# A sliding-window attention with a gated network: w_out folded in quarters, more transposes given to the DMA queues

## The chip, the cores and the metric

One core of a Trainium2 chip runs the kernel. The metric is the device time of one execution in microseconds (us), the median of several runs. TensorE (PE) multiplies matrices, VectorE (DVE) and ScalarE (ACT) copy and compute element by element, GpSimd (POOL) issues the loads that change type from float32 to bfloat16, and SyncE (SP) issues plain transfers and DMA transposes. All transfers share 16 DMA engines. Matrix results land in PSUM and are copied from there to SBUF.

## The reference, cut to what matters

Four batches, eight heads, 768 positions, head size 64. Attention keeps the first four positions (the sinks) and a window of 128; its output, heads side by side, is a 3072 x 512 matrix x. Two projections of x are multiplied with each other, then go through two more matrices:

```
keep = is_sink | in_window
scores = np.where(keep, scale * q @ k.T, -1e9)
a = softmax(scores)
x = (a @ v).transpose(0, 2, 1, 3).reshape(B * S, H * D)
h = (x @ w1) * (x @ w2) @ w3
out = h @ w_out
```

w1 and w2 are 512 x 1024, w3 is 1024 x 1024, w_out is 1024 x 512.

## The kernel before, in words

**The fold.** w3 @ w_out is made once on the core, as w3o (1024 x 512), so that each token row costs one projection. For each of the eight 128-row blocks i of w3, task t3.i (L381) turns the block on TensorE, copies it to w3t, and tasks fm.i.n (L392) multiply it with a column half n of w_out and copy the result (tile pw) to w3o. Three w3 blocks come as raw float32 through SP (L162, the names say "ab" because they lie in that buffer); they are transposed in float32, in two halves of four. The other five and w_out come through POOL as bfloat16.

**Attention.** A unit is a batch b, a pair of heads r and a tile t of 256 rows. q and k have to be turned so that the head dimension lies on partitions: batch 0 on TensorE from a layout of row pairs (tpq, tpk, L240), batch 1 on TensorE (L219), batches 2 and 3 by DMA transposes issued on SP, one per 128 rows (tdq, tdk, L249). sc.b.r.t multiplies (L288), ACT takes the exponential, DVE multiplies with the mask; av.b.r.t multiplies with v (L322), DVE divides. The sinks' scores for all heads are made in one go (sp, L282) with the first unit of a tile: in batch 0 for each tile on its own (256 columns), in batches 1 to 3 once for tiles 1 and 2 together (512 columns). The attention output xn is turned to xT: on TensorE for batches 0 and 1 (xt, L339), by DMA transposes for 2 and 3 (xd, L349).

**Network.** g.b.c.dt.half multiplies xT with a 128-column block of w1 (half 0, ACT copies it) or w2 (half 1, DVE multiplies the two into ab), for a chunk c of 256 (batch 0) or 384 tokens (L362). p.b.m multiplies 128 rows of ab with w3o (L402), a copy goes to o_sb, one of three buffers, and SP stores it (L409). The last of all projections is cut into pieces of 256, 128 and 128 columns, which are copied and stored apart (L419 to L426).

**What sets the order.** Each engine works in program order. TensorE's order is the string PLAN, task by task. The order on ACT, DVE and SP is found while the kernel is built, by a small planner with fixed costs and arrival times for the loads; a task marked "any" goes to whichever of DVE and ACT it reckons free first. The loads on POOL are in the list `order`, with the making of the identity matrices and masks between them (at places 2, 6 and 8 of the list); at most eight of POOL's loads are under way. Ahead of the first load TensorE multiplies zeros (keep_busy, tile pz), so many times as the planner sees room for. Every instruction waits for semaphores of what it reads, and everything behind it on its engine waits with it. PSUM has four buffers for all tasks but scores, which have two of their own.

```
order = [("wo", 256, 512), ("q", 0, 0), ("k", 0, 0), ("w3", 3), ("w3", 4), ("w3", 6), ("wo", 0, 256), ...
for n in (0, 1) if i < HALVED else (None,):
    me = ("fm", i, n)
    n0, n1 = (0, DM) if n is None else (256 * n, 256 * n + 256)
```

Of the kernel before, what the change touches and what calls it, by code (L numbers as in the profile page):

```python
# [21 lines left out]
def kernel(  # L22
# [31 lines left out]
    XPOSE = (2, 3)  # L54
    X_XPOSE = (2, 3)
# [3 lines left out]
    RAW = (("w3", 0), ("w3", 1), ("w3", 2))  # L59
# [62 lines left out]
    def load(what, *i):  # L122
# [18 lines left out]
        else:  # L141
# [5 lines left out]
    order = [("wo", 256, 512), ("q", 0, 0), ("k", 0, 0), ("w3", 3), ("w3", 4), ("w3", 6), ("wo", 0, 256), ("k",  # L147
             0, 1), ("v", 0, 0), ("q", 0, 1), ("w3", 5), ("w3", 7), ("w1", 0, 256), ("k", 0, 2),
             ("v", 0, 1), ("w2", 256, 512), ("w2", 0, 256), ("q", 0, 2), ("w1", 256, 512), ("w2",
             512, 768), ("w1", 512, 768), ("w1", 768, 1024), ("w2", 768, 1024), ("v", 0, 2)] + [  # L150
# [3 lines left out]

    def raw(i):
        return ab[0][:].rearrange("p k s -> p (k s)")[:, i * 2048:(i + 1) * 2048].bitcast(FP32)

    raw_at = {}
    for n, x in enumerate(RAW):
        raw_at[x] = raw(n)  # L160
        if x[0] == "w3":
            nc.sync.dma_start(out=raw(n), in_=moe_w3[x[1] * P:(x[1] + 1) * P, :])  # L162
        else:
            nc.sync.dma_start(out=raw(n).rearrange("p (h x) -> p h x", h=H), in_=pairs({"q": q, "k": k}[x[0]], *x[1:]))
# [61 lines left out]
    def cast(x):  # L226

        dst = {"q": qN, "k": kN}[x[0]][x[1]]
        out = dst[:, 2 * x[2]:2 * x[2] + 2, :].rearrange("p i n -> p (i n)")
        (nc.vector.tensor_copy if x[0] == "k" else nc.scalar.copy)(out, raw_at[x])  # L230
        yield
# [180 lines left out]
    def project_pieces(b, m):  # L412
# [10 lines left out]
        for i, (n0, n1) in enumerate(PIECES):  # L423
            o_sb = work.tile([P, n1 - n0], FP32, tag=f"o_{i}", bufs=1, name="o_sb")
            (nc.scalar.copy if i == 1 else nc.vector.tensor_copy)(o_sb[:], pos[i][:])
            (nc.scalar if i == 1 else nc.sync).dma_start(out=out[t0:t0 + P, n0:n1], in_=o_sb[:])  # L426
# [13 lines left out]
    def pieces(what, *i):  # L440
        if what == "qkv":
            for kb in range(i[1], i[2]):
                for x in "kqv":
                    slow = 0.9 if i[0] in XPOSE and x != "v" else 0.0
                    yield 0.25 * 1.35 + slow * RATE, 256, [(x, i[0], kb)]
# [6 lines left out]
        elif what == "w3":  # L452
            yield 0.475, 4096, [("w3", i[0])]
        elif what == "wo":
            yield 1.03 * (i[1] - i[0]) / 256, 1024, [("wo", n) for n in range(i[0] // 256, i[1] // 256)]
        else:
            yield 1.03 * (i[1] - i[0]) / 512, 1024, [(what, n) for n in range(i[0] // P, i[1] // P)]

    streams = [[[0.8 + RAW_US * n + 1.2, 0.475 if x[0] == "w3" else 0.555, 4096 if x[0] == "w3" else 512,
                 [("raw",) + x]] for n, x in enumerate(RAW)],  # L460
# [32 lines left out]
    for key in arrive:  # L493
        if key[0] in ("k", "q", "v"):
            arrive[key] += (0.0, 0.3, 1.0, 4.0)[key[1]]
# [3 lines left out]
    XP_US, XX_US, LATE_US = 9.0, 7.5, 12.0  # L499
    PLAN = """  # L500
        t3.0.0 t3.0.4 t3.1.0 t3.1.4 t3.2.0 t3.2.4 fm.0.1 fm.1.1 fm.2.1 tpq.0.0.2 tpq.0.0.0 tpk.0.0.0
        tpk.0.0.2 t3.3.0 sc.0.0.0 sc.0.1.0 t3.4.0 fm.3.1 t3.6.0 sc.0.2.0 sc.0.3.0 fm.4.1 fm.6.1 fm.3.0
        fm.0.0 tpk.0.1.0 tpk.0.1.2 fm.4.0 sv.0 fm.1.0 av.0.0.0 av.0.1.0 fm.2.0 tpq.0.1.2 tpq.0.1.0
        t3.5.0 xt.0.0.0 av.0.2.0 sc.0.0.1 sc.0.1.1 av.0.3.0 fm.5.0 fm.5.1 t3.7.0 tpk.0.2.0 tpk.0.2.2
        sc.0.2.1 sc.0.3.1 fm.7.0 av.0.0.1 av.0.1.1 xt.0.2.0 fm.7.1 fm.6.0 xt.0.0.1 av.0.2.1 g.0.0.0.0
        g.0.0.0.1 av.0.3.1 g.0.0.1.0 g.0.0.1.1 g.0.0.2.0 xt.0.2.1 g.0.0.2.1 tpq.0.2.2 tpq.0.2.0
        g.0.1.1.0 g.0.1.2.0 g.0.1.0.0 g.0.1.0.1 sc.0.0.2 sc.0.1.2 g.0.1.2.1 g.0.1.1.1 g.0.0.5.0
        g.0.1.4.0 g.0.1.5.0 g.0.1.4.1 g.0.0.5.1 g.0.1.3.0 g.0.1.6.0 g.0.1.6.1 sc.0.2.2 sc.0.3.2 av.0.0.2
        av.0.1.2 g.0.1.3.1 g.0.1.5.1 g.0.0.4.0 tpk.1.0 g.0.1.7.0 g.0.0.6.0 g.0.0.4.1 xt.0.0.2 tpq.1.0
        av.0.2.2 g.0.0.3.0 g.0.1.7.1 sc.1.0.0 sc.1.1.0 sv.1 g.0.0.6.1 p.0.2 tpq.1.1 av.0.3.2 g.0.0.3.1  # L510
        g.0.0.7.0 g.0.0.7.1 sc.1.2.0 sc.1.3.0 xt.0.2.2 av.1.0.0 tpk.1.1 p.0.0 g.0.2.4.0 tpq.1.2
        g.0.2.5.0 g.0.2.1.0 g.0.2.1.1 av.1.1.0 p.0.1 av.1.2.0 g.0.2.4.1 g.0.2.2.0 av.1.3.0 g.0.2.2.1
        sc.1.0.1 sc.1.1.1 xt.1.2.0 g.0.2.5.1 g.0.2.3.0 g.0.2.7.0 g.0.2.7.1 g.0.2.0.0 g.0.2.0.1 g.0.2.3.1
        g.0.2.6.0 tpk.1.2 sc.1.2.1 sc.1.3.1 g.0.2.6.1 p.0.3 av.1.0.1 av.1.1.1 av.1.2.1 sc.1.0.2 sc.1.1.2
        p.0.5 xt.1.0.1 av.1.3.1 sc.1.2.2 sc.1.3.2 xt.1.0.0 p.0.4 xt.1.2.1 av.1.0.2 av.1.1.2 sc.2.0.0
        sc.2.1.0 av.1.2.2 g.1.0.4.0 g.1.0.4.1 xt.1.0.2 g.1.0.0.0 av.1.3.2 g.1.0.6.0 g.1.0.6.1 xt.1.2.2
        g.1.0.2.0 g.1.0.2.1 g.1.0.0.1 g.1.1.6.0 g.1.0.1.0 g.1.1.1.0 g.1.1.1.1 g.1.1.6.1 g.1.0.5.0
        g.1.0.5.1 av.2.0.0 av.2.1.0 sc.2.2.0 sc.2.3.0 g.1.0.1.1 g.1.0.3.0 g.1.0.3.1 g.1.1.7.0 g.1.1.7.1
        av.2.2.0 g.1.1.5.0 sc.2.0.1 sc.2.1.1 g.1.1.5.1 av.2.3.0 g.1.1.2.0 g.1.1.2.1 g.1.1.3.0 g.1.1.0.0
        g.1.1.0.1 g.1.0.7.0 g.1.0.7.1 sv.2 sc.2.2.1 sc.2.3.1 g.1.1.3.1 p.1.2 av.2.0.1 av.2.1.1 av.2.2.1  # L520
        g.1.1.4.0 g.1.1.4.1 av.2.3.1 sc.2.0.2 sc.2.1.2 p.1.4 p.1.3 sc.2.2.2 sc.2.3.2 av.2.0.2 av.2.1.2
        p.1.5 sc.3.0.0 sc.3.1.0 p.1.1 av.2.2.2 av.2.3.2 sc.3.2.0 sc.3.3.0 p.1.0 g.2.0.7.0 g.2.0.5.0
        g.2.0.5.1 g.2.0.2.0 av.3.0.0 g.2.0.2.1 g.2.0.7.1 g.2.0.4.0 g.2.0.4.1 g.2.0.1.0 g.2.0.1.1 sv.3
        g.2.0.3.0 g.2.0.3.1 g.2.0.6.0 g.2.0.6.1 av.3.1.0 sc.3.0.1 sc.3.1.1 g.2.1.3.0 g.2.1.3.1 av.3.2.0
        g.2.1.7.0 g.2.1.4.0 g.2.1.2.0 g.2.1.2.1 av.3.3.0 g.2.1.7.1 g.2.1.5.0 sc.3.2.1 sc.3.3.1 g.2.1.4.1
        g.2.1.1.0 g.2.1.1.1 g.2.1.6.0 av.3.0.1 av.3.1.1 sc.3.0.2 sc.3.1.2 av.3.2.1 av.3.3.1 g.2.1.5.1
        g.2.0.0.0 g.2.0.0.1 sc.3.2.2 sc.3.3.2 g.2.1.6.1 p.2.2 p.2.0 av.3.0.2 av.3.1.2 av.3.2.2 av.3.3.2
        g.2.1.0.0 g.2.1.0.1 p.2.1 p.2.5 g.3.0.5.0 g.3.0.5.1 g.3.0.0.0 g.3.0.6.0 g.3.0.3.0 g.3.0.0.1
        g.3.0.4.0 g.3.0.4.1 g.3.0.3.1 p.2.4 g.3.0.6.1 g.3.1.1.0 g.3.1.1.1 g.3.1.5.0 g.3.1.3.0 g.3.1.5.1
        g.3.1.6.0 g.3.0.1.0 g.3.0.1.1 g.3.1.6.1 g.3.1.3.1 g.3.1.0.0 g.3.1.0.1 g.3.1.7.0 g.3.1.7.1  # L530
        g.3.1.2.0 g.3.0.2.0 g.3.0.2.1 g.3.0.7.0 g.3.0.7.1 g.3.1.2.1 g.3.1.4.0 g.3.1.4.1 p.3.2 p.3.3
        p.3.4 p.3.0 p.3.1 p.3.5 p.2.3
    """

    def task(name, prio, gen, stages, after=(), loads=(), ring=None, started=(),
# [6 lines left out]
    w3_home = [{("t3", x[1], j): (2048 * n, 2048 * n + 2048) for n, x in enumerate(RAW) if x[0] == "w3"  # L542
                for j in (0, 4)}, {("t3", i, 0): (n * DF, n * DF + DF) for n, i in enumerate(BF_W3) if n < 6}]
    for n, x in enumerate(RAW):
        if x[0] != "w3":
            w3_home[0]["cast", x[0]] = (2048 * n, 2048 * n + 2048)
    for i in range(KFF):
# [9 lines left out]
        for n in (0, 1) if i < HALVED else (None,):  # L557
            me = ("fm", i, n)
            folded.append(me)
            n0, n1 = (0, DM) if n is None else (256 * n, 256 * n + 256)  # L560
# [3 lines left out]
                 t3, ([("wo", 0)] if n != 1 else []) + ([("wo", 1)] if n != 0 else []), "mm")  # L564
    def xn_free(b, t):
        b, t = (b, t - 2) if t == 2 else (b - 1, t + 1)
        return [] if b < 0 else ([("xd", b, t, i) for i in range(2)] if b in X_XPOSE else
# [3 lines left out]
    for b in range(B):  # L571
        for t in range(NT):
# [3 lines left out]
            for n, src, dst in (("k", kN[b], kT[b]), ("q", qN[b], qT[b])):  # L576
                if b in XPOSE:
                    for kb in kbs:
                        qk.append(("td" + n, b, kb))
                        task(qk[-1], 1, transposes_dma(src, dst, kb), [("sp", 1.4), ("dma", XP_US)],  # L580
                             war, [(n, b, kb)],
                             late=[("tp" + n, b - 2, t, r0) for r0 in (0, 2)] if b - 2 in PAIRED else
                             [("tp" + n, b - 2, t)])
# [11 lines left out]
                else:  # L595
                    qk.append(("tp" + n, b, t))
                    task(qk[-1], 1, transposes(src, dst, t), [("pe", 0.447), ("dve", 0.69)],
                         [], [(n, b, kb) for kb in kbs], "mm")
# [6 lines left out]
            for r in range(NP):  # L605
# [5 lines left out]
                if t > 0 and r == 0 and (b == 0 or t == 1):  # L611
                    sinks = (t, t + 1) if b == 0 else (1, NT)
                    after.append(("sk", b))
                    if b > 0:
                        after += [("tdq", b, 4), ("tdq", b, 5)] if b in XPOSE else [("tpq", b, 2)]
# [14 lines left out]
                if not lead and b not in X_XPOSE:  # L630
                    task(("xt", b, r - 1, t), 2.5, x_transposes(b, r - 1, t),
                         [("pe", 0.224), ("any", dict(dve=0.69, act=0.6))],
                         [("av", b, r - 1, t), ("av", b, r, t)], [], "mm")
            if b in X_XPOSE:
                for i in range(2):
                    task(("xd", b, t, i), 1, x_transposes_dma(b, t, i), [("sp", 1.3), ("dma", XX_US)],
# [209 lines left out]
```

## Time and profile before

| | us |
|---|---|
| median of 6 runs | 198.9 (198.12 to 199.43) |
| the profiled execution | 198.12 |
| its span in the trace | 196.4 |
| TensorE busy | 188.0 (96%) |
| VectorE, ScalarE busy | 117.2 and 102.6 |
| share of q0 (loads from POOL) of the 16 DMA engines | 91.7% |
| share of q1 (SP: raw loads, transposes, stores) | 30.9% |

The span runs from the first to the last instruction of the trace; the 1.7 us between it and the execution's time lie around it. Busy time counts overlapping instructions once. A line names source line, engine and operation, then what is written and read; "us to landing" is the time from a DMA's issue to its completion. The chain of work that ended last follows the last instruction back, at each step to what it waited for; its pieces are start, length and what ran.

### The profile page before, as it was taken

The page shows a single profiled execution, that of the slowest core. Times are in us where ns is not written, and L with a number is a line of the kernel's source. Part 1 is how long each engine was busy: PE and PEld are TensorE (multiplying, and loading weights), DVE is VectorE, ACT ScalarE, POOL GpSimd, SP SyncE. Part 2 cuts the span into 40 slices and gives each one's busy share as a digit, 9 for nine tenths or more (in the row PEclk, how much of TensorE's full clock was granted, in tenths as well). Part 3 has the DMA queues.
Part 4 walks back from the last instruction along what each step waited for, and adds up shares of the span by engine and source line. Part 5 has one row for each costly group of instructions (what it writes and reads, how often), then busy time and mean ns, then how long its engine had stood idle before and what let it go on. Part 6 is the DMA issues. An engine that isn't in the chain of part 4 may idle for free.

```text
span 196.4 us, 4629 instructions
## 1 busy us (share of the span) xinstructions
PE 188.0 (96%) x1858; PEld 125.8 (64%) x1870; DVE 117.2 (60%) x278; ACT 102.6 (52%) x174; POOL 71.9 (37%) x96
## 2 busy tenths in 40 slices
PE   6699999999999999999999999999999999999993
PEld 2577788888867686766655655556565655665442
DVE  5446477756887778684757766665687523254112
ACT  2338378468545477973566466526865332423210
POOL 7972666679999855242781000000000000000000
PEclk9999999999999999999999999999999999999999
DMA  6999999999999999999999999920212330100233
GB/s 216 234 199 194 182 185 186 197 170 155 155 154 181 180 145 158 152 205 146 155 155 132 156 168 245 154 80 0 29 27 73 118 134 0 58 0 0 104 146 124
DMA packets 99445, 26.77 MB, mean 136 GB/s; under 512 B 88928, under 2 KB 95456, under 8 KB 99424
## 3 DMA queue, kind: packets, MB, share of 16 engines
q0 software_dynamic: 75664, 13.90, 91.7%
q1 hardware_dynamic: 23616, 12.52, 30.9%
q8 instruction: 14, 0.23, 0.5%
q10 hardware_dynamic: 144, 0.07, 0.1%
q14 instruction: 7, 0.06, 0.1%
HBM read 29.36 MB, written 6.29 MB: 182 GB/s over the span
## 4 chain that ended last, share of the span: by engine, by line
PE 88%; DMA 6%; POOL 3%; issue 1%; DVE 0%; POOLq 0%
PE pg L362 43%; PE po L402 20%; PE av L322 8%; DMA wo_sb<-in_moe_w_out_dram 6%; PE sc L288 6%; PE pw L392 5%; PE xt L339 2%; PE tp L219 1%; PE tp L240 1%; PE po L419 1%; POOL ab L129 1%; PE sp L282 1%; POOL wo_sb L119 1%; PE tp L381 1%; PE vp L263 0%
## 5 line engine op out<-in xcount | busy, mean ns | idle before, releaser
L362 PE MATMUL pg<-xT,w_sb 128*128 128x384 bf16 (+1 forms) x576 | 89.7, 308 | 0.0
L362 PEld LDWEIGHTS <-w_sb 128*128 128x128 bf16 x576 | 54.2, 98 | 26.5 <-issue 1.3
L366 DVE TENSOR_TENSOR ab<-a_sb,pg 128x384 bf16<-128x384 f32 (+1 forms) x72 | 36.4, 509 | 34.7 <-PE pg L362 32.5
L369 ACT COPY a_sb<-pg 128x384 f32<-128x384 f32 (+1 forms) x72 | 31.9, 444 | 38.2 <-PE pg L362 28.4
L296 ACT ACTIVATE ex<-sc 128x1024 bf16<-128x1024 f32 (+1 forms) x48 | 43.9, 955 | 7.9 <-PE sc L288 7.7
L402 PE MATMUL po<-w3o,ab 128*128 128x512 bf16 x172 | 41.4, 379 | 0.6
L300 DVE TENSOR_TENSOR am<-ex,maskt 128x1024 bf16<-128x1024 bf16 (+1 forms) x48 | 29.8, 640 | 2.2 <-ACT ex L296 2.0
L402 PEld LDWEIGHTS <-ab 128*128 128x128 bf16 x184 | 17.5, 98 | 19.5 <-issue 0.5
L212 ACT COPY o_sb<-po 128x512 f32<-128x512 f32 x17 | 10.0, 585 | 23.0 <-PE po L402 22.9
L329 DVE TENSOR_TENSOR xn<-av,rec 128x256 bf16<-128x256 f32 x48 | 20.4, 424 | 1.6
L113 POOL DMA_DIRECT2D qN<-in_q_dram x18 | 16.1, 895 | 9.5 <-DMA vN<-in_v_dram 8.2
L113 POOL DMA_DIRECT2D vN<-in_v_dram x18 | 16.1, 892 | 8.6 <-DMA kN<-in_k_dram 7.1
L322 PE MATMUL av<-vN,am 128*128 128x65 bf16 x352 | 18.5, 193 | 0.0
L322 PEld LDWEIGHTS <-am 128*128 128x128 bf16 x352 | 16.8, 97 | 2.1 <-issue 0.2
L113 POOL DMA_DIRECT2D kN<-in_k_dram x18 | 16.1, 894 | 4.9 <-DMA qN<-in_q_dram 4.4
L392 PE MATMUL pw<-wo_sb,w3t 128*128 128x256 bf16 x128 | 15.6, 273 | 2.1 <-DMA wo_sb<-in_moe_w_out_dram 2.1
L392 PEld LDWEIGHTS <-w3t 128*128 128x128 bf16 x128 | 12.0, 98 | 4.3 <-DMA wo_sb<-in_moe_w_out_dram 1.7
L288 PE MATMUL sc<-qT,kT 64*128 64x128 bf16 (+1 forms) x256 | 13.9, 238 | 0.0
L326 DVE RECIPROCAL rec<-av 128x4 f32<-128x4 f32 x48 | 8.5, 177 | 8.0 <-PE av L322 7.6
L322 PE MATMUL av<-vs,es 128*128 128x130 bf16 x64 | 12.2, 220 | 0.0
L212 DVE COPY o_sb<-po 128x512 f32<-128x512 f32 x6 | 4.1, 692 | 11.9 <-PE po L402 8.8
L288 PEld LDWEIGHTS <-kT 64*128 64x128 bf16 x256 | 8.2, 94 | 4.5 <-issue 3.2
(70 smaller groups left out, 121.9 us busy)
## 6 DMA issues: line engine op xcount, KB each, us to landing
out_dram<-o_sb SPq DMA_DIRECT2D x23, 256.0 KB, 2.4
vN<-in_v_dram POOLq DMA_DIRECT2D x24, 128.0 KB, 9.5
kN<-in_k_dram POOLq DMA_DIRECT2D x18, 128.0 KB, 9.1
qN<-in_q_dram POOLq DMA_DIRECT2D x18, 128.0 KB, 9.5
w_sb<-in_moe_w_dram POOLq DMA_DIRECT2D x8, 256.0 KB, 9.6
ab<-in_moe_w_dram SPq DMA_DIRECT2D x3, 512.0 KB, 4.2
ab<-in_moe_w_dram POOLq DMA_DIRECT2D x5, 256.0 KB, 10.7
wo_sb<-in_moe_w_out_dram POOLq DMA_DIRECT2D x2, 512.0 KB, 10.5
```

The costliest lines, as they stand in the source:

```text
L113: nc.gpsimd.dma_start(out=dst, in_=rows(src, b, kb))
L212: (nc.scalar.copy if home[me] == "act" else nc.vector.tensor_copy)(dst, src)
L288: nc.tensor.matmul(sc[:, e, c:c + n], kT[b][hp, r, kb * P:(kb + 1) * P], qT[b][hp, r, qb * P:qb * P + n], start=True, stop=True)
L296: nc.scalar.activation(ex[:, :, c0:], sc[:, :, c0:], ACTF.Exp, scale=scale)
L300: nc.vector.tensor_mul(am[:, :, c0:], ex[:, :, c0:], mk)
L322: nc.tensor.matmul(o, lhs, rhs, start=(n == 0), stop=(n == len(todo) - 1), skip_group_check=True)
L329: nc.vector.tensor_mul(xns[b, t][:, :, r, :, :], av[:, :, :, 0:D], rec[:].to_broadcast([P, 2, 2, D]))
L362: nc.tensor.matmul(pg[:], w_sb[:, kk, dt * P:(dt + 1) * P], xT[b][:, kk, tk], start=(kk == 0), stop=(kk == NP - 1))
L366: nc.vector.tensor_mul(ab[b][:, dt, tk], gate_a.pop((b, c, dt))[:], pg[:])
L369: nc.scalar.copy(a_sb[:], pg[:])
L392: nc.tensor.matmul(po[:], w3T[i][:, j, :], wo_sb[:, j, n0:n1], start=(j == 0), stop=(j == KFF - 1))
L402: nc.tensor.matmul(po[:], ab[b][:, kk, m * P:(m + 1) * P], w3o[:, kk, :], start=(kk == 0), stop=(kk == KFF - 1))
```

## The change

Five things change together.

- w_out is loaded in four quarters of 128 columns (`CUTS`) instead of two halves, and each fold task fm.i.n makes 128 columns instead of 256: 32 tasks of 8 matmuls instead of 16. The functions that load, multiply and copy are the same; a path for loading w_out raw is added but not taken, as `RAW` is unchanged.
- Tile 2 (rows 512 to 767) of batch 1: q and k are turned by four DMA transposes on SP instead of 16 matmuls and two copies, and x by two DMA transposes instead of 8 matmuls and two copies.
- The sinks of batch 1 are made for tiles 1 and 2 apart, 256 columns each, as in batch 0.
- The list `order` and PLAN are others. The first loads are now two quarters of w_out and two w3 blocks; the first transposes are of the second raw w3 block; attention of batch 0 begins after more of the fold. The number of filler matmuls goes from 6 to 12: nine ahead of the first transposes, and three after the first fold task. The planner's arrival times and DMA costs are other numbers.
- In the last projection DVE copies the first two pieces and ACT the third (before: DVE, ACT, DVE), and the stores follow the three copies, two on SP and the third on ACT.

On SP the order becomes: three raw loads; the four transposes of batch 1; then transposes of batch 2 with stores of batch 0 between them; the two x transposes of batch 1 after batch 2's ninth q or k transpose; the last three of batch 2; then batch 3's with batch 1's stores and batch 2's x transposes.

```diff
-    XPOSE = (2, 3)
-    X_XPOSE = (2, 3)
+    XPOSE = [(1, 2), (2, 0), (2, 1), (2, 2), (3, 0), (3, 1), (3, 2)]
+    X_XPOSE = [(1, 2), (2, 0), (2, 1), (2, 2), (3, 0), (3, 1), (3, 2)]
+    CUTS = (0, 128, 256, 384, 512)
+    SPLIT = (0, 1)
...
-    order = [("wo", 256, 512), ("q", 0, 0), ("k", 0, 0), ("w3", 3), ("w3", 4), ("w3", 6), ("wo", 0, 256), ("k",
-             0, 1), ("v", 0, 0), ("q", 0, 1), ("w3", 5), ("w3", 7), ("w1", 0, 256), ("k", 0, 2),
...
+    order = [("wo", 384, 512), ("wo", 128, 256), ("w3", 5), ("w3", 4), ("wo", 0, 128), ("q", 0, 0), ("k", 0, 0),
+             ("w3", 3), ("wo", 256, 384), ("v", 0, 0), ("k", 0, 1), ("q", 0, 1), ("w3", 7), ("w3",
+             6), ("w1", 256, 512), ("q", 0, 2), ("k", 0, 2), ("v", 0, 1), ("w2", 256, 512), ("w1",
...
-        for i, (n0, n1) in enumerate(PIECES):
-            o_sb = work.tile([P, n1 - n0], FP32, tag=f"o_{i}", bufs=1, name="o_sb")
-            (nc.scalar.copy if i == 1 else nc.vector.tensor_copy)(o_sb[:], pos[i][:])
-            (nc.scalar if i == 1 else nc.sync).dma_start(out=out[t0:t0 + P, n0:n1], in_=o_sb[:])
+        o_sbs = [work.tile([P, n1 - n0], FP32, tag=f"o_{i}", bufs=1, name="o_sb") for i, (n0, n1) in enumerate(PIECES)]
+        for i in range(3):
+            (nc.scalar.copy if i == 2 else nc.vector.tensor_copy)(o_sbs[i][:], pos[i][:])
+        turn = (len(RAW) + 2 * 2 * len(XPOSE) + 2 * len(X_XPOSE) + B * NB - 1) % 8
+        for i in {7: (2, 0, 1), 6: (0, 2, 1), 5: (0, 1, 2)}.get(turn, (0, 1, 2)):
+            n0, n1 = PIECES[i]
+            (nc.scalar if i == 2 else nc.sync).dma_start(out=out[t0:t0 + P, n0:n1], in_=o_sbs[i][:])
...
     PLAN = """
-        t3.0.0 t3.0.4 t3.1.0 t3.1.4 t3.2.0 t3.2.4 fm.0.1 fm.1.1 fm.2.1 tpq.0.0.2 tpq.0.0.0 tpk.0.0.0
-        tpk.0.0.2 t3.3.0 sc.0.0.0 sc.0.1.0 t3.4.0 fm.3.1 t3.6.0 sc.0.2.0 sc.0.3.0 fm.4.1 fm.6.1 fm.3.0
...
+        t3.1.4 t3.0.4 t3.2.0 t3.0.0 t3.1.0 t3.2.4 fm.0.3 fm.1.1 fm.2.1 fm.2.3 t3.5.0 fm.0.1 fm.1.3
+        t3.4.0 fm.5.1 fm.5.3 fm.1.0 fm.4.0 fm.5.0 fm.2.0 fm.0.0 fm.4.1 tpq.0.0.0 tpq.0.0.2 tpk.0.0.2
+        tpk.0.0.0 fm.4.3 t3.3.0 sc.0.0.0 sc.0.1.0 fm.2.2 fm.5.2 sv.0 fm.3.0 fm.3.1 sc.0.2.0 sc.0.3.0
...
-        for n in (0, 1) if i < HALVED else (None,):
+        for n in range(len(CUTS) - 1):
             me = ("fm", i, n)
             folded.append(me)
-            n0, n1 = (0, DM) if n is None else (256 * n, 256 * n + 256)
+            n0, n1 = CUTS[n], CUTS[n + 1]
...
-                if b in XPOSE:
+                if (b, t) in XPOSE:
                     for kb in kbs:
...
-                if t > 0 and r == 0 and (b == 0 or t == 1):
-                    sinks = (t, t + 1) if b == 0 else (1, NT)
+                if t > 0 and r == 0 and (b in SPLIT or t == 1):
+                    sinks = (t, t + 1) if b in SPLIT else (1, NT)
...
-                if not lead and b not in X_XPOSE:
+                if not lead and (b, t) not in X_XPOSE:
                     task(("xt", b, r - 1, t), 2.5, x_transposes(b, r - 1, t),
...
-            if b in X_XPOSE:
+            if (b, t) in X_XPOSE:
                 for i in range(2):
```

## The prediction

> **What bounds the kernel now.** I read the page first, for which engine fills the span.
>
> ```profile
> span 196.4 us, 4629 instructions
> PE 188.0 (96%) x1858; PEld 125.8 (64%) x1870; DVE 117.2 (60%) x278; ACT 102.6 (52%) x174; POOL 71.9 (37%) x96
> PE   6699999999999999999999999999999999999993
> DMA  6999999999999999999999999920212330100233
> ```
>
> TensorE is full except in the first two slices and the last. The DMA engines are full as well, until about 130 us. The chain that ended last shows where each of the two sets the pace:
>
> ```profile
> 7.49 12.57 DMA wo_sb<-in_moe_w_out_dram
> 20.06 0.04 issue
> 20.10 1.91 PE pw L392 x16
> ...
> 51.32 0.22 PE xt L339 x4
> 51.55 0.45 PE tp L219 x8
> ...
> 67.17 0.33 PE sp L282 x4
> ...
> 72.31 0.55 PE sc L288 x12
> 72.86 0.54 PE pg L362 x4
> ...
> 191.29 1.78 PE po L419 x24
> ```
>
> From 20.10 us on the chain is TensorE alone, back to back, up to 193.07 us; a tail of 3.3 us (copy, store, landing) follows. So a microsecond of TensorE work taken out after 20 us is a microsecond of the end, as long as no new wait opens. Before 20 us the loads set the pace. TensorE's timeline there:
>
> ```profile
> 4.36 3.98 PE L381 MATMUL tp<-ident,ab 128*128 128x128 f32 x24 [0.29 <-DMA ab<-in_moe_w_dram]
> 9.84 2.79 PE L392 MATMUL pw<-wo_sb,w3t 128*128 128x256 bf16 x24 [1.51 <-DMA wo_sb<-in_moe_w_out_dram]
> 13.93 0.62 PE L381 MATMUL tp<-ident,ab 128*128 128x128 bf16 x8 [0.28 <-DMA ab<-in_moe_w_dram]
> 15.25 0.62 PE L381 MATMUL tp<-ident,ab 128*128 128x128 bf16 x8 [0.26 <-DMA ab<-in_moe_w_dram]
> 20.10 1.91 PE L392 MATMUL pw<-wo_sb,w3t 128*128 128x256 bf16 x16 [0.62 <-DMA wo_sb<-in_moe_w_out_dram]
> ```
>
> Four waits for loads, 2.67 us, the largest for the first half of w_out.
>
> **What the Trainium skill says.** "TensorE: Matmul & The Clock Gate", Part 1, gives one matmul every N/2.4 + 2.5 ns once warm and half the clock before that, with a warm-up of about 3.4 us of activity. The trace agrees: 24 matmuls of 16x128 and 8x256 columns take 1.78 us on the chain (55.6 and 109 ns each make 1.76), and 8 of the 24 fp32 transposes start between 4.30 and 6.05 us, 213 ns apart, the next ones 109 ns. "DMA: Bandwidth & Descriptors", Specifications, puts full rate at 512 bytes a transfer and more. Here q0 moved about 760 packets of 512 bytes in 16 to 18 us (380 a us) and 1427 mostly of 256 bytes in 10 to 12 us (714 a us): 195 against 183 GB/s, a small loss. "Advanced Engine Details and Errata", X-Bar Transpose, calls DMA transposes as fast as regular DMAs. For landing on a busy queue the trace decides: 8.2 and 8.5 us in 62 to 92 us, where plain loads take 12 to 14.
>
> **The change, part by part.**
>
> *Transposes of batch 1, last 256 rows.* TensorE loses 16 matmuls (tp L219, 0.45 per 8) and 8 (xt L339, 0.22 per 4): 0.90 + 0.44 = -1.34 us. Their copies leave DVE and ACT, neither of which is on the chain: nothing.
>
> *Sinks of batch 1 per tile.* One 512-column set of 4 (0.33) becomes two of 256 (0.22 each, the length that batch 0's has): +0.11 us; each holds one change of tile shape, about 0.1 us (0.55 against 0.44 for sc). Over the whole built order such changes go from 62 to 63, this one alone.
>
> *Fold in quarters.* 128 matmuls of 256 columns become 256 of 128: 256 x 55.6 - 128 x 109.2 = +0.26 us. Sixteen more PSUM copies, but 265 to 292 ns each on two engines (the last tile's 128-column copies) against one fold task per 0.44 us: hidden under TensorE; without that cover they would cost 16 x 0.28 = 4.5 us shared by two engines.
>
> So the work after the start shrinks by 1.34 - 0.11 - 0.26 = 0.97 us.
>
> *w_out in quarters, start.* POOL has two more loads to issue, about 0.9 us each; q0 is loaded 6 to 12 us deep by then, so that is hidden (bare, it would delay each later load by 1.8 us). A half takes 1024/380 = 2.7 us of queue time, a quarter 1024/714 = 1.43, so w_out takes 5.7 instead of 5.4, and loads behind it are 0.3 later. The three raw w3 blocks land 3.4, 4.2 and 5.4 us after their issues (4.2, 5.5, 7.1 us), and q0 hardly moves before 5.8 us (7 packets in 4.0 to 5.8). First quarter: about 8.6 us (half: 9.8). Then +1.43 for a quarter, q or k (q 11.2, k 12.7 now), +1.27 for a w3 block, +0.85 for v. In the new order: wo 8.6, wo 10.05, w3 11.3, w3 12.6, wo 14.05, q 15.5, k 16.95, w3 18.2, wo 19.65, v 20.5 and 21.3, up to 0.7 later at the end, as the second half is now.
>
> TensorE against this: nine filler matmuls end at 5.2 (six now at 4.07), and the first transposes need the second raw block: start 5.6 instead of 4.36. That is less bad than it looks, as only 2 or 3 then run cold instead of 8. Third block at 7.26 as now, transposes end at 9.1. One quarter (0.45), three fillers (0.64), then fm.1.1 at 10.15, w3 block 5 at 11.5, block 4 at 12.8, fm.1.0 at 14.15, q at 16.8, k at 17.5, block 3 about 18.8, first scores done at 19.8. At full clock that work is 24 x 0.109 + 120 x 0.056 + 24 x 0.056 + 1.1 + 0.55 = 12.3 us, so 7.5 us are lost, and with some 0.6 for the fourth quarter and v just behind, 8.1. Now, up to 20.10: 24 x 0.109 + 48 x 0.109 + 24 x 0.056 + 1.1 + 1.1 = 11.4, so 8.7 lost. Gain 0.6 us; with loads 0.7 us later than I take them it is nothing or slightly negative, with loads always ahead 1.2.
>
> *Last tile.* Same matmuls; ACT instead of DVE copies the last 128 columns (265 against 292 ns) and stores from its own queue, 1.7 us to landing on both. Nothing; bounds -0.1 to +0.3.
>
> *The DMA transposes and SP's queue.* SP now issues four transposes of batch 1 ahead of the first store, and two of x in the middle of batch 2's. Each costs SP 1.2 to 1.7 us. Batch 1's rows 512 to 767 landed from 56.2 (k) to 59.7 us (q); issued at 57 to 61, transposed by 70; the scores that read them come at about 74.5 on TensorE. Covered by 4 us. The stores of batch 0 wait behind them, but the first is ready only at 65. On the shared engines a transpose takes the place of about 0.75 us of loads (in 76 to 78 us q1 moved 726 packets, mostly of transposes, and q0 1108, against 2339 in 54 to 56 us: 1231 packets given up, 1.05 us, for 726; I take a transpose for 512 of 256 bytes, its 128 KB). So batch 2's loads end some 3 us later, batch 3's 4.5. Batch 2's last q transpose (issued 86.6, landed 94.4, first read at 99.1) also stands behind the two x transposes, which wait for attention of batch 1 at 84: I get 90.7 + 7.8 = 98.5, read at 101. Batch 2's second x tile, behind batch 3's k transposes: 113 + 6.5 = 119.5, read at 121.8 (now 120.3 and 123.8). Each cover shrinks from about 4 us to about 2.4. If both hold, nothing; if one fails by 1 or 2 us, that much is paid at once, because scores and gates stand in TensorE's fixed order with the projections behind them. I take 0.2 as the expected small loss.
>
> *The rest of the order.* Gates, scores and projections are dealt out anew, in the same shapes. I cost that at nothing: ACT and DVE, at 52 and 60%, hide it. If a copy stands in a wrong place, TensorE waits for it, 0 to 1 us in all; a gain is not to be had, since no wait of TensorE is left after 20 us to remove.
>
> **Sum.** 0.97 + 0.6 - 0.2 = 1.4 us: span 196.4 to 195.0, the profiled execution 198.12 to 196.7. It was the fastest of six; on the median 198.9 the same step gives 197.5 us, -0.7%. No change can be told within about 0.5%, 1.0 us.
>
> **Rivals.** *The start is bound by loads and gains nothing* (chance 0.28): several steps above come within 0.3 us of their landing. For it speaks that the second half of w_out took 3.6 us beyond its predecessor rather than 2.7; against it that q0's order now brings a usable piece every 1.3 us. Then 0.97 less some 0.5 of waits: 198.4 us. *The DMA transposes become the bound* (0.17): batch 2's last q transpose lands late at the first scores of its second tile. Cover 2.5 us; slower by more than 1.0 us needs a landing 2.5 + 1.4 + 1.0 = 4.9 us later than 98.5. For it speak 14.3 us to landing for loads in 62 to 92 us and a full DMA row; against it that loads are only half of what SP waits for. At 5.5 us late TensorE waits 3.0: 197.5 + 3.0 = 200.5 us. *The start runs free of loads and nothing stalls*: 0.97 + 1.2, 196.7 us, in the first case's range.
>
> **Chances and range.** The forecast, 0.55 (its own range 196.5 to 197.9); no gain at the start, 0.28; transposes bound, 0.17. Faster 0.55, same 0.28, slower 0.17. Range 196.6 to 200.0.
>
> **What would show it.** First fp32 transposes at 5.6 us, first fold matmul near 9.1, the waits between 9 and 22 us under 1.5 us in total; TensorE back to back from 22 us; a wait for qT or xT near 101 or 122 us would show the second rival. I am wrong if TensorE's work is not about 1 us smaller, if the quarters land later than 8.6 and 10, or if stores behind SP's transposes hold back the output copies.

## The result, and the profile after

The changed kernel takes 199.95 us (median of 20 runs, 198.66 to 203.16), the kernel before 198.71 (41 runs measured beside it). The ratio is 1.0049, 95% interval 1.0029 to 1.0068: about 1 us slower, where the prediction had 1.4 us faster. The profiled execution took 201.61 us with a span of 199.9, so it is one of the longer ones; what it shows is larger than in the median run. Ratios leave out executions more than 1.5% above the fastest of the same kernel and medians keep them: three executions of the changed kernel are left out, and below, 15 of 22 with batch 3's loads later and seven of 22 with the other start.

The page of the changed kernel, first the engines' shares in 40 slices of 5 us:

```profile
span 199.9 us, 4881 instructions
PE 190.2 (95%) x1973; PEld 127.2 (64%) x1984; DVE 118.6 (59%) x282; ACT 102.8 (51%) x183; POOL 73.8 (37%) x98
PE   7899999999999999999999997599999999999993
```

TensorE is full but for the first two slices, the last, and two from 120 to 130 us. The last two are new. TensorE's waits from 22 us to the end (total, times, longest) say what it waited for there:

```profile
PE pg L383 <- ACT o_sb L226: 2.1, 1, 2.1
PE pg L383 <- DMA xT<-xn: 1.0, 1, 1.0
```

The chain of work that ended last, in that place (start, length, what ran):

```profile
119.56 7.21 DMA out_dram<-o_sb
...
127.13 0.59 ACT o_sb L226
...
127.77 2.72 PE pg L383 x8
130.49 0.66 PE av L343 x12
```

A store that SP issued at 119.56 us landed 7.2 us later; ScalarE waited for it with a copy into the same output buffer, and TensorE waited for that copy. Just before, at 123.0, TensorE had already waited 1.0 us for xT of batch 2. Then eight gate matmuls take 2.72 us. The same piece takes 1.30 us in the kernel of 197.3 us below, so TensorE's clock had dropped to half: the granted clock is 0.50 from 127.75 to 131.10 us, and 1.00 before and after. The Trainium skill ("TensorE: Matmul & The Clock Gate", Part 1) says that an idle window of about 3.4 us halves the clock; here waits of 1.0 and 2.1 us were enough. Waits 3.1 and slow matmuls (2.72 - 1.30) + (0.66 - 0.37) = 1.7 make 4.8 us; these are called the hole below. Without them the span is 195.1 us, and 195.0 was predicted.

The clock does not fall in every execution. Of the 21 on record, six have a mean granted clock of 0.99, as this one; the other 15 have 0.998 or more and a median of 199.73 us. So the kernel is slower at full clock too. Median and ratio miss the prediction by 2.4 to 2.6 us; if all of that is the hole, it is usually about half of the one shown.

The start went nearly as foretold. TensorE's timeline there:

```profile
5.71 1.06 PE L402 MATMUL tp<-ident,ab 128*128 128x128 f32 x8 [0.56 <-DMA ab<-in_moe_w_dram]
7.21 1.97 PE L402 MATMUL tp<-ident,ab 128*128 128x128 f32 x16 [0.43 <-DMA ab<-in_moe_w_dram]
9.09 0.62 PE L413 MATMUL pw<-wo_sb,w3t 128*128 128x128 bf16 x8
...
20.54 0.84 PE L413 MATMUL pw<-wo_sb,w3t 128*128 128x128 bf16 x12 [0.36 <-DMA wo_sb<-in_moe_w_out_dram]
```

First fp32 transposes at 5.71 (5.6 predicted), first fold matmul at 9.09 (9.1); the five waits for loads of before, 2.96 us (the prediction's 2.67 leaves out the first), have become four of 1.61 us: these three, and 0.26 us for batch 0's first k at 17.9.

What is late in the hole is batch 2's second x tile. In the trace SP issued its two transposes at 116.39 and 118.20 us, and they landed at 124.01 and 125.44. Ahead of them SP stood until 115.10 for a k transpose of batch 3, whose load landed at 115.09; in the kernel before the same load landed at 105.22. SP's issues there, first before, then after (start, length, what):

```profile
108.42 1.34 SPq L249 DMA_TRANSPOSE kT<-kN  x1
...
113.22 4.50 SPq L349 DMA_TRANSPOSE xT<-xn  x2
```

```profile
115.10 1.19 SPq L270 DMA_TRANSPOSE kT<-kN  x1
116.39 3.08 SPq L370 DMA_TRANSPOSE xT<-xn  x2
119.56 0.53 SPq L430 DMA_DIRECT2D out_dram<-o_sb  x1
```

The first line of each is the transpose of that same load. The store that ScalarE's copy waited for had its data at 114.4 us, but stands right behind the x tile on SP, so both waits of the hole follow from SP's wait for the late load.

### The profile page after: what moved, and what is told of

Read it like the earlier page. It is cut to its first block, busy times and chain, and to the rows that moved or that the text cites. A ratio compares the mean times of both kernels' runs of the same rounds, so it can differ in the third digit from the quotient of the medians.

```text
span 199.9 us, 4881 instructions
## 1 busy us (share of the span) xinstructions
PE 190.2 (95%) x1973; PEld 127.2 (64%) x1984; DVE 118.6 (59%) x282; ACT 102.8 (51%) x183; POOL 73.8 (37%) x98
## 4 chain that ended last, share of the span: by engine, by line
PE 83%; DMA 9%; POOL 4%; issue 1%; ACT 1%; POOLq 0%; ACTq 0%
PE pg L383 42%; PE po L423 18%; PE av L343 7%; PE sc L309 6%; DMA wo_sb<-in_moe_w_out_dram 5%; PE pw L413 4%; DMA out_dram<-o_sb 4%; POOL wo_sb L121 1%; PE xt L360 1%; PE tp L261 1%; PE po L440 1%; PE tp L233 1%; POOL ab L131 1%; PE sp L303 1%; PE tp L402 1%
## 5 line engine op out<-in xcount | busy, mean ns | idle before, releaser
L383 PE MATMUL pg<-xT,w_sb 128*128 128x384 bf16 (+1 forms) x576 | 91.8, 311 | 3.1 <-ACT o_sb L226 2.1
L226 ACT COPY o_sb<-po 128x512 f32<-128x512 f32 x18 | 10.5, 585 | 25.9 <-PE po L423 19.4
L343 PE MATMUL av<-vN,am 128*128 128x65 bf16 x352 | 19.3, 195 | 0.0
L413 PE MATMUL pw<-wo_sb,w3t 128*128 128x128 bf16 x256 | 16.3, 219 | 0.4 <-DMA wo_sb<-in_moe_w_out_dram 0.4
L413 PEld LDWEIGHTS <-w3t 128*128 128x128 bf16 x256 | 14.6, 98 | 1.5 <-DMA wo_sb<-in_moe_w_out_dram 0.6
L226 DVE COPY o_sb<-po 128x512 f32<-128x512 f32 x5 | 3.5, 691 | 9.8 <-PE po L423 6.9
(69 smaller groups left out, 123.0 us busy)
```

The lines of the kernel that those rows point to most:

```text
L226: (nc.scalar.copy if home[me] == "act" else nc.vector.tensor_copy)(dst, src)
L343: nc.tensor.matmul(o, lhs, rhs, start=(n == 0), stop=(n == len(todo) - 1), skip_group_check=True)
L383: nc.tensor.matmul(pg[:], w_sb[:, kk, dt * P:(dt + 1) * P], xT[b][:, kk, tk], start=(kk == 0), stop=(kk == NP - 1))
L413: nc.tensor.matmul(po[:], w3T[i][:, j, :], wo_sb[:, j, n0:n1], start=(j == 0), stop=(j == KFF - 1))
```

## The experiments

The kernel before ran beside all of them: 198.7 to 199.0 us. Each ratio is to it, with its 95% interval. Theory and rival are named in each expectation.

**Six output buffers.**

```diff
-        o_sb = work.tile([P, DM], FP32, tag="o_sb", name="o_sb")
+        o_sb = work.tile([P, DM], FP32, tag="o_sb", bufs=6, name="o_sb")
```

> The changed kernel with six output buffers (o_sb) instead of three, nothing else; the order on every engine is the same. Theory A (batch 1's stores stand in SP's order behind transposes that wait for late loads, the three output buffers are all taken, ACT stops at a copy and the gates behind it stop TensorE): the copy no longer waits, the 4.5 us wait of ACT for a store is gone, what stays is about 1 us of waiting for xT of batch 2; span about 196 to 196.5, time 197.8 to 198.2, ratio to the kernel before 0.995 to 0.998. Theory B (xT of batch 2 is late because the DMA queues are full, and the output buffers only happen to be full at the same time): TensorE waits for xT as long as before, ratio 1.002 to 1.006.

Measured: 201.53 us, ratio 1.0114 (1.0061 to 1.0166). The wait for the output copy is gone; TensorE's waits after 22 us are now headed by

```profile
PE pg L383 <- DMA xT<-xn: 3.8, 2, 2.4
```

and 0.5 us for a gate's copy. The buffers only stood in front of the x tiles, which are late themselves. The second and the third x tile of batch 2 were each waited for. Whether more buffers made it slower than the change (1.0049, 1.0029 to 1.0068) is not certain, as the intervals touch; in this profile the start, too, was 1.2 us later.

**Batch 1's stores on ScalarE's queue.**

```diff
-        nc.sync.dma_start(out=out[t0:t0 + P, :], in_=o_sb[:])
+        (nc.scalar if b == 1 else nc.sync).dma_start(out=out[t0:t0 + P, :], in_=o_sb[:])
```

> The changed kernel with the six stores of batch 1 issued by ACT right behind their copies instead of by SP; SP's order is otherwise the same, and ACT spends about 0.4 to 0.5 us more per store. Theory A, with SP's order as the cause: stores leave within 1 us of the copy, land 6 to 7 us later, and the fourth copy (8 us after the first) finds a buffer; ratio 0.994 to 0.999. Theory A', with the long landing as the cause rather than SP's order: ACT still waits for 1 us or more, ratio about 1.001. Theory B: ratio 1.002 to 1.006.

Measured: 203.63 us, ratio 1.0207 (1.017 to 1.0244). ScalarE stood at stores that it had to issue, the last two until about 130 us, and TensorE waited for ScalarE (2.8 us for a gate's copy, 2.5 for an exponential). ScalarE's timeline there:

```profile
129.82 0.90 ACTq L430 DMA_DIRECT2D out_dram<-o_sb  x2
130.76 0.86 ACT L390 COPY a_sb<-pg 128x384 f32<-128x384 f32 x2 [4.28 <-DMA qT<-qN]
```

The wait ended when a k and a q transpose of batch 3, issued by SP at 121.6 and 123.0, landed at 129.75 and 130.23, and the stores read neither. In the trace the transfers of SP and ScalarE take turns on eight semaphores, and each of these two stores waited for the one that the transpose had held. So what held ScalarE was the slow landing of SP's transposes, through a shared semaphore; that the full queue itself would hold a store back is not shown. The blockage moved to an engine that TensorE needs more.

**Batch 3's k and q later in the planner's books**, so that SP takes batch 2's second x tile earlier.

```diff
-            arrive[key] += (0.0, 0.3, -0.5, 2.0)[key[1]]
+            arrive[key] += (0.0, 0.3, -0.5, 9.0)[key[1]]
```

> The changed kernel with the planner told that batch 3's loads come 7 us later; TensorE's order is the same, SP now issues the stores and x transposes of batches 1 and 2 ahead of more of batch 3's k and q transposes. Theory A: neither the stores nor the second x tile of batch 2 wait behind a transpose that waits for its load; both waits near 123 to 128 us go, span 195 to 195.7, time 196.8 to 197.4, ratio 0.989 to 0.994. Theory C (the loads themselves come too late for the attention of batch 3, so only the place of the wait moves): a wait of 2 us or more for qT or kT of batch 3, ratio above 1.0.

Measured: median 201.42 us, single executions from 197.58 to 204.19, ratio 1.0006 (0.9971 to 1.0041); with so wide a spread it is open whether this is better than the change. In the profile the second x tile was issued at 114.6 and 115.8 and landed without a wait; TensorE then waited 1.7 us for the third x tile, which stood behind a store and landed at 132.8. So the order on SP decides which tile is late; here the next one was.

**The change without batch 1's six transposes.**

```diff
-    XPOSE = [(1, 2), (2, 0), ...
-    X_XPOSE = [(1, 2), (2, 0), ...
+    XPOSE = [(2, 0), ...
+    X_XPOSE = [(2, 0), ...
```

(and the tasks tpq.1.2, tpk.1.2, xt.1.0.2 and xt.1.2.2 back in PLAN)

> The changed kernel with q, k and x of batch 1's last tile transposed on TensorE again (the four tasks put back into the order; w_out, fold, sinks and loads as changed). TensorE has 1.34 us more to do; six DMA transposes fewer. Theory A: batch 2's and 3's loads land 5 to 10 us earlier, no wait near 123 us; span 195.0 + 1.3 = 196.3, time 198.0, ratio 0.995 to 0.998. Theory D (the new order of gates, scores and projections makes the wait, not the six transposes): loads earlier but the wait stays, ratio 1.005 to 1.01. The last load's landing against 129.1 us in the changed kernel gives the price of six transposes: 4.5 us by the prediction's 0.75 us each, 10 us if they make the whole difference to the kernel before (118.9).

Measured: 198.46 us, ratio 0.9983 (0.9961 to 1.0004). TensorE has no wait after 22 us, and the last v of batch 3 lands at 120.7 us instead of 129.1. So without the six the order has no hole. Its work after the start is, by the prediction's sums, 0.26 + 0.11 = 0.37 us more than before, and yet it is 0.3 us faster: if all of that is the start's, the new start is worth about 0.7 us (0.3 to 1.1 by the interval; 0.6 predicted). But its profiled execution lost time there: the third raw w3 block landed at 8.46 us, not 7.2, and the transposes after that wait ran at half clock:

```profile
8.51 3.38 PE L402 MATMUL tp<-ident,ab 128*128 128x128 f32 x16 [1.88 <-DMA ab<-in_moe_w_dram]
```

3.38 us for 16 of them, 1.97 us in the changed kernel's profile.

**The kernel before with the six transposes alone.** Its TensorE order, halves and start kept; transposes early on SP.

```diff
-    XPOSE = (2, 3)
-    X_XPOSE = (2, 3)
+    XPOSE = [(1, 2), (2, 0), ...
+    X_XPOSE = [(1, 2), (2, 0), ...
...
-            arrive[key] += (0.0, 0.3, 1.0, 4.0)[key[1]]
+            arrive[key] += (0.0, -10.0, 1.0, 9.0)[key[1]]
```

> The kernel before, its TensorE order, its w_out in halves and its start kept, with the six DMA transposes of batch 1's tile 2 (and its sinks per tile) alone; they stand early on SP, and the x transposes of batch 2 stand ahead of more of batch 3's. TensorE has 1.34 - 0.11 = 1.2 us less to do. Theory (a DMA transpose takes 1.4 to 1.6 us of the loads' time, and what is late then is x of batch 2): the last v of batch 3 lands at 126 to 129 us in the trace instead of 118.9, and TensorE waits between 110 and 135 us for one of xT, qT or kT, 0.5 to 2.5 us: between 198 and 199.5 us against 198.9. Rival (a transpose takes the 0.75 us that the prediction gave it; what cost the time is the new order and the start): last v at 122 to 124 us, no wait, 197.7 us, a ratio of 0.994.

Measured: 209.64 us, ratio 1.054 (1.0504 to 1.0576), 10 us above either expectation. The chain shows the one cause:

```profile
85.76 3.27 PE pg L382 x20
...
89.62 1.41 SPq L369
...
91.08 7.85 DMA xT<-xn
...
98.97 1.14 PE pg L382 x3
```

Here it is batch 1's own x tile. In the order of before, the gates that read it come soon after its attention, which is no harm for a transpose on TensorE (0.22 us) and 10.0 us of waiting for two DMA transposes that take 7.9 us to land. So the transposes needed another order of tasks than that of before. The last v of batch 3 landed early, at 117.1: the halt made batch 2's attention late, SP stood for it from 104 to 113.8 us, and many of batch 3's transposes came after the loads. So this run speaks for neither price of a transpose.

**Order and covers given back, at one go.** Second x tile of batch 2 ahead of all but one of batch 3's transposes (9.0 above is 16.0), six output buffers, all gates of batch 2's first chunk ahead of the second's.

```diff
-            arrive[key] += (0.0, 0.3, -0.5, 2.0)[key[1]]
+            arrive[key] += (0.0, 0.3, -0.5, 16.0)[key[1]]
...
-        ... g.2.0.3.0 g.2.0.3.1 g.2.1.7.0 g.2.1.7.1 g.2.0.6.1 g.2.1.1.0 g.2.0.0.0 ...
+        ... g.2.0.3.0 g.2.0.3.1 g.2.0.6.1 g.2.0.0.0 g.2.0.0.1 g.2.0.5.0 g.2.0.4.0 ...
```

> The changed kernel with the same transposes on the queues, but SP's order and the slack given back: batch 2's second x tile ahead of all but one of batch 3's transposes, output buffers six instead of three, and the gates of batch 2's second chunk after all of its first. The loads still pay for six transposes. Theory (the loss is the hole of 5 us at 118 to 131 us, which is a matter of order and not of TensorE's work): TensorE has no wait over 0.4 us after 22 us, last v of batch 3 still lands at 126 to 129 us, span about 195.5, time 196.6 to 197.6 us, a ratio of 0.989 to 0.993. Rival (the loads' lateness itself is the loss, wherever SP puts the transposes): the wait moves to batch 3's q, k or v or to another x tile, and the time stays at 199 us or above.

Measured: 207.57 us, ratio 1.0434 (1.0403 to 1.0465); the rival was right. No x tile was late, but TensorE's waits begin with

```profile
PE sc L309 <- DMA qT<-qN: 5.2, 1, 5.2
```

SP waited from 103.5 to 112.7 us for batch 2's attention, with batch 3's q behind the x tile: the second was issued at 120.4 and landed at 122.9, and the scores that read it were due at 117.8. The last v landed at 119.9, not at 126 to 129, as most of batch 3's transposes came later: here the loads were early, and still something was late.

**Four transposes instead of six**: batch 1's last x tile on TensorE again, in the order of the change.

```diff
-    X_XPOSE = [(1, 2), (2, 0), ...
+    X_XPOSE = [(2, 0), ...
```

> The changed kernel with batch 1's last x tile turned on TensorE again (0.44 us more work): four DMA transposes more than before instead of six. Theory (1.4 to 1.6 us of load time each): last v of batch 3 lands at 125.5 to 127.5 us, between 120.7 without any and 129.1 with six; TensorE's wait for batch 2's x tile shrinks to 0 to 1.5 us; 198.0 to 199.3 us. Rival (the two x transposes, in the middle of batch 2's on SP, are what costs): last v near 122 us, no wait, 197.6 us.

Measured: 199.91 us, ratio 1.004 (1.002 to 1.006). Last v at 126.0 us, as the theory had it; the wait for the x tile is gone, the one for the output copy is 1.6 us. The median is above both expectations (the profiled execution, 198.87 us, is not): fewer transposes alone don't close the hole. In the trace SP still waited until 111.8 and 113.8 us for batch 3's k and q, with batch 2's x tile and the store behind them.

**A start that needs the third raw block later**, without the six transposes.

```diff
-        t3.1.4 t3.0.4 t3.2.0 t3.0.0 t3.1.0 t3.2.4 fm.0.3 ...
+        t3.1.4 t3.0.4 t3.0.0 t3.1.0 t3.2.0 t3.2.4 fm.0.3 ...
```

> The changed kernel without batch 1's six DMA transposes (they are on TensorE again), and with the four half blocks that come from the first and second raw block turned first, the third raw block fifth instead of third. Theory (part of the start is lost in executions in which the third raw block lands after 8 us, as it did in four of the six traces so far): no wait over 0.6 us before the first fold matmul, TensorE at full clock from about 7 us, and about 0.5 us less than the same kernel with the old order of these tasks (198.46): 197.9 us, a ratio of 0.995. Rival (the loads behind the raw blocks set the start anyway): 198.4 us, with the wait moved to w_out's first quarters.

Measured: 198.2 us, ratio 0.9975 (0.9957 to 0.9993). The third block landed at 7.7 us and cost nothing; no wait after 22 us. With the old order of these tasks the ratio was 0.9983, so the difference itself is within the intervals.

**Order on SP, buffers, start, with four and with six transposes.** Two kernels that differ only in X_XPOSE, as above: first with four.

```diff
-            arrive[key] += (0.0, 0.3, -0.5, 2.0)[key[1]]
+            arrive[key] += (0.0, 0.3, -0.5, 9.0)[key[1]]
```

with six buffers, the start above, and all gates of the chunk moved.

> The changed kernel with batch 1's last x tile on TensorE again (four DMA transposes more than before), the first and second raw block turned ahead of the third, six output buffers, batch 2's second x tile on SP ahead of all but five of batch 3's q and k transposes, and the gates of batch 2's second chunk after its first. Theory (the more of batch 3's transposes get in ahead of the last load, the later everything lands; with x early on SP and the two covers widened nothing is late): last v of batch 3 at 123 to 126 us, no wait of TensorE over 0.4 us after 22 us, span 195.2 to 196.0, 197.0 to 197.7 us, ratio 0.991 to 0.995. Rival (something else becomes late in turn, as the q of batch 3 did where all its transposes stood behind x): a wait of 1 us or more between 110 and 135 us, and 198.5 us or above.

Measured: 199.43 us, ratio 1.0028 (1.0013 to 1.0043). Then with six.

> As the one with four transposes, with all six of the change. Theory: 0.44 us less TensorE work than with four, loads some 2 us later; if the widened covers hold, span 194.8 to 195.6 and 196.6 to 197.3 us; the chance of that is even, since x of batch 2 would still land 7 to 8 us after its issue. Rival (six are too many for the queue, whatever the order): a wait of 1 us or more between 110 and 135 us and 198.5 us or above.

Measured: 199.56 us, ratio 1.0026 (1.0006 to 1.0045). In both the hole near 120 us is closed, no transfer is waited for after 22 us. But moving all gates changed the orders on ScalarE and VectorE: a gate's copy stands ahead of an exponential at 141 us, and a gate's product ahead of a mask at 148. The waits of the kernel with four:

```profile
PE av L343 <- DVE am L321: 1.2, 1, 1.2
PE sc L309 <- ACT ex L317: 1.1, 1, 1.1
```

These 2.3 us are the experiment's own. The kernel with six has the same two, and 0.7 us for another copy at 102 us.

**The other start on the changed kernel alone.**

```diff
-        t3.1.4 t3.0.4 t3.2.0 t3.0.0 t3.1.0 t3.2.4 fm.0.3 ...
+        t3.1.4 t3.0.4 t3.0.0 t3.1.0 t3.2.0 t3.2.4 fm.0.3 ...
```

> The changed kernel with one edit: the four half blocks of the first and second raw w3 block are turned first, the third raw block fifth instead of third. Theory (the start's exposure to the third raw block and the hole near 120 us add up): the spread of single executions above 201 us gets smaller and the median falls by 0.3 to 0.8 us, to 199.2 to 199.7 us, with the hole of some 3 to 5 us still there. Rival (the start has no part in it): 199.9 us and the same spread.

Measured: 200.7 us (198.39 to 202.4), ratio 1.006 (1.0035 to 1.0085). The hole is there unchanged (2.1 us for the output copy, 1.3 for xT), and neither median nor spread fell: the rival holds, this start does not narrow the spread.

**Only three gates moved.** As the two above, but only g.2.0.6.1, g.2.0.0.0 and g.2.0.0.1 ahead of the second chunk, so that ScalarE and VectorE keep the order of the run with arrival offset 9.0.

```diff
-        ... g.2.1.7.0 g.2.1.7.1 g.2.0.6.1 g.2.1.1.0 g.2.0.0.0 g.2.1.1.1 g.2.1.4.0 g.2.1.2.0 g.2.0.0.1 ...
+        ... g.2.0.6.1 g.2.0.0.0 g.2.0.0.1 g.2.1.7.0 g.2.1.7.1 g.2.1.1.0 g.2.1.1.1 g.2.1.4.0 g.2.1.2.0 ...
```

> The changed kernel with all six of its DMA transposes, x of batch 2 early on SP, six output buffers, the first two raw blocks turned first, and only three gates of batch 2's first chunk moved ahead of its second chunk, which leaves the order on ScalarE and VectorE as in the changed kernel. Theory (the hole of about 5 us was all that stood between the prediction and the result; the 2.3 us of waits at 141 us in the run with all gates moved came from that move): no wait above 0.5 us at 115 to 145 us, span 195.2 to 196.0, 196.9 to 197.7 us, ratio 0.991 to 0.995. Rival (with six transposes some load or transpose is late whatever the order): a wait of 1 us or more for a transfer, 198.7 us or above.

Measured with six: 198.74 us, ratio 0.9987 (0.9966 to 1.0008). TensorE waits 2.5 us for xT in all, 1.7 of it for batch 2's third x tile, which was issued at 127.56 and 128.99 and landed at 133.53 and 133.98. The rival holds for this order. It does not hold for every one: with all gates moved, six transposes left no transfer late, but the copies cost more.

> The same with batch 1's last x tile on TensorE, four DMA transposes more than before. Theory: 0.44 us more TensorE work than with six and no wait of TensorE over 0.4 us: span 195.4 to 196.0, 197.1 to 197.7 us, ratio 0.991 to 0.995. Rival: a wait of 1 us or more for a transfer or for a copy between 110 and 145 us, 198.5 us or above.

Measured with four: 197.3 us (6 runs, 196.61 to 197.94), ratio 0.9922 (0.9896 to 0.9949), faster than both kernels. The theory holds for the sum of the edits; which of them are needed (four transposes, SP's order, buffers, start, gates) was not tried one by one. TensorE has no wait after 22 us, and the chain passes the place of the hole like this:

```profile
124.25 1.30 PE pg L383 x8
125.55 0.18 PE av L343 x6
125.73 1.30 PE pg L383 x8
127.03 0.37 PE av L343 x12
```

**Six transposes that nobody reads.** The kernel without batch 1's six and with the start above (198.2 us), plus six into spare buffers, at the place of the change's first four on SP.

```diff
+    spare = [const.tile([P, NP, P], BF16, name=f"spare_{i}") for i in range(6)]
+    def transposes_spare(i):
+        src, kb = ((kN, qN, kN)[i // 2][1], 4 + i % 2)
+        nc.sync.dma_start_transpose(out=spare[i][:], in_=src[:, kb, :])
+        yield
```

> The kernel without batch 1's six transposes and with the first two raw blocks turned first (198.2 us, last v of batch 3 at 122.0 us), and with six DMA transposes added that nobody reads: batch 1's last k, q and k again into spare buffers, at the place of the change's first four on SP. TensorE's work and order are untouched; extra work is done that the reference doesn't need. Theory (a DMA transpose that lands ahead of the last load takes 1.2 to 1.6 us of the loads' time, and a later end of the loads lets more of batch 3's transposes in ahead of it): last v of batch 3 at 129 to 132 us, 29 to 31 transposes landed ahead of it instead of 23, and a hole near 120 us of 2 to 6 us: 199.5 to 202 us. Rival (0.75 us each as predicted; the changed order of the tasks made the hole): last v at 126 to 127 us, no hole, 198.2 to 198.6 us.

Measured: 203.34 us, ratio 1.0221 (1.019 to 1.0251), above the theory's range; about 5 us for transposes without a reader, on a TensorE order without a hole. Its chain:

```profile
122.62 5.38 DMA xT<-xn
...
128.05 2.74 PE pg L390 x8
```

The picture is that of the changed kernel, with the half clock: SP stood until 119.87 us for a k load of batch 3, with batch 2's second x tile behind it. TensorE, ScalarE, VectorE and GpSimd work in the same order in both kernels; on SP the six are added, and a few stores of batch 0 stand elsewhere. So six more transposes are enough to open the hole in this order of tasks, without a reader and without a change on TensorE. That order itself is part of the picture, as it sets how early a late tile is read; no run shows whether six would open it in the order of before. The landing, however, was the rival's: last v at 127.0.

Landings in the traces (us), and how many DMA transposes landed ahead of the last load:

| kernel | last k of batch 2 | fourth k of batch 3 | last v of batch 3 | transposes |
|---|---|---|---|---|
| before | 84.8 | 105.2 | 118.9 | 22 |
| change without the six | 83.1 | 105.1 | 120.7 | 23 |
| the same, other start | 86.4 | 107.2 | 122.0 | 23 |
| the same, six unread | 92.4 | 112.5 | 127.0 | 29 |
| changed kernel | 92.6 | 115.1 | 129.1 | 30 |
| four, order of the change | 92.1 | 111.8 | 126.0 | 28 |
| four, 197.3 us | 92.4 | 108.8 | 121.6 | 24 |

Six unread transposes move the loads by 6.0, 5.3 and 5.1 us, 0.85 to 1.0 each. The six of the change move them by 6.2 to 7.9 us against the kernel with the other start, and by 8.4 to 10.0 against the one with the old start: 1.0 to 1.7 each. With the change seven more transposes landed ahead of the last load than in either, not six: loads that end later let more of batch 3's transposes, and stores, in before them. That this feeds back is an inference from these counts; no run held the count fixed. Why the last kernel's loads end 4.6 us earlier than those of the run with all gates moved (126.2), with the same orders on SP and POOL, stays open; each is one trace.

## Why the prediction was wrong, point by point

- *TensorE work 0.97 us less; start 0.6 us better; sum 195.0 us of span.* Borne out in sum, partly by luck. The first six loads landed within 0.1 us of their predicted times (first quarter 8.68, q 15.50), those from k on 0.8 to 0.9 us later (k at 17.88 instead of 16.95), and the change without its transposes gives a start worth 0.7 us. The span less the hole is 195.1. But TensorE's last matmul, less the hole, ends 0.9 us earlier than before, where the sum gives 1.4; the tail behind it, priced at nothing, took 3.0 us in this trace instead of 3.35. For the kernel of 197.3 us the same sum, with 0.44 us for the x tile back on TensorE and the start at its measured 0.7, gives 0.97 - 0.44 + 0.7 = 1.2 us; measured 1.5 (1.0 to 2.1).
- *A transpose takes the place of about 0.75 us of loads; batch 2's loads end 3 us later, batch 3's 4.5.* Mis-sized. 0.85 to 1.0 us by the unread ones; in the changed kernel batch 2's last k was 7.8 us later than before, and batch 3's 9.9 us halfway and 10.2 at the end.
- *Batch 2's second x tile: 113 + 6.5 = 119.5, read at 121.8.* This step failed. SP reached it at 116.4 and 118.2, because the load that had landed at 105 before now landed at 115 and SP waited for it with the x transposes behind; landing took 7.2 to 7.6 us, so the tile was there at 125.4, 5.9 us late against a cover of 2.4. The prediction itself counted loads 4.5 us late, but left the x transposes at 113, where SP reached them before (113.2), as if SP's waits did not move with the loads.
- *I take 0.2 as the expected small loss.* It was 4.8 us in the profile, and about half of that in the median. The waits were priced one for one ("that much is paid at once"); in this execution the clock added 1.7 us to 3.1, in 15 of 21 it added next to nothing.
- *I am wrong if stores behind SP's transposes hold back the output copies.* They did: 2.1 us of the 3.1 in the profile, for the store right behind the x tile. It was named but had no price in the sum.
- *Rival: the DMA transposes become the bound*, 200.5 us, chance 0.17. This is what happened, near its time (199.95) and in another place: batch 2's last q landed at 102.4 us and cost 0.2 at most, the x tile 20 us later and the store behind it cost the rest.
- *Rival: start bound by loads.* Not so in the median, though in the traces where the third raw block landed at 8.0 to 8.7 us TensorE waited 0.8 to 2.0 us there, and twice ran at half clock afterwards.
- *The rest of the order, nothing.* In the changed kernel's profile the one copy that was waited for, 2.1 us, was late through its store and not through its place. How little it takes is shown by the kernels with all gates moved: 2.3 us for a copy ahead of an exponential and a product ahead of a mask.

## What to carry to other kernels

Before work is moved from a full engine to a full DMA queue, move every landing behind it, and every wait of the queue's issuing engine with the landings; then compare each tile with its first reader, above all those that stand behind other waits on the issuing engine. A DMA transpose that saves little (0.2 us of TensorE per 128 rows here) needs a reader 7 to 9 us or more away under such loads, so the order of the reader has to change with it. A wait of the full engine is dearer than its length when the clock follows (1.7 us on top of 3.1 in one execution).

## What the runs showed of the hardware

- In the changed kernel the 30 DMA transposes of 128 x 512 bf16 that landed ahead of the last load took 7.1 to 9.2 us from issue to landing (median 8.1), and the eight issued after it 2.3 to 4.5; stores of 256 KB took 6.3 to 7.4 us beside the loads. The Trainium skill ("Advanced Engine Details and Errata", X-Bar Transpose) calls such transposes as fast as regular DMAs. What an unread one costs the loads, 0.85 to 1.0 us for 128 KB, is about as much as a v load of that size takes at the start (0.85 us), so this agrees: on the shared engines it costs about as much as one more load.
- Waits well under 3.4 us can halve TensorE's clock. In the traces, single waits of 1.9, 2.0, 2.4, 2.5 and 2.8 us were each followed by half clock, one of 2.5 us (stores on ScalarE, at 118 us) was not, and none of up to 1.75 us that stood alone was. So length alone does not decide it. The half clock then lasted 3.4 us; after waits of 5.2 and 10.0 us it lasted 6.8 and 10.2, part of it within the wait.
- The third raw block's load, issued at 1.73 us, landed between 7.1 and 8.7 us: 8.0 to 8.7 in the first four experiments, 7.7 to 8.2 in the next four, 7.1 to 7.4 in the next three, 7.9 to 8.5 in the last three. Each group ran one after the other on one chip. The first and the third group ran on the same one, with kernels that issue the same loads up to this one, so neither the kernel nor the chip alone explains it.
